# Converting float64 weights on chip in 512-column pieces, in place, with w_in's column groups as tiles of their own

## The chip, the cores and the metric

The kernel runs on one core of one Trainium2 chip. The metric is the device time of one execution in microseconds, as the median of several runs. A core has TensorE (PE in the profile), VectorE (DVE), ScalarE (ACT), GpSimd (POOL) and SyncE (SP), which here issues all transfers.

## The reference, cut to what matters

```python
def _attn_ref(q, k, v):                 # q, k, v: 8 batches, 8 heads, 576 positions, 64 columns, float32
    scores = scale * np.matmul(q, k.transpose(0, 1, 3, 2))
    mask = block_i >= block_j           # blocks of 64 positions
    scores = np.where(mask, scores, -1e9)
    ...                                 # softmax over the last axis
    return np.matmul(attn, v)

def _moe_ref(x, w_in, w_out):           # x: 4608 x 512, w_in: 512 x 2048, w_out: 2048 x 512
    h = x @ w_in
    g = np.where(h >= 1, h, np.where(h <= -1, 0.0, (h + 1) ** 2 / 4))
    return g @ w_out
```

x is the attention's result with the heads side by side. The two weight matrices come in as float64, 64 bits an element; q, k and v are float32.

## The kernel before

**Arithmetic.** TensorE multiplies operands of a rounded 32-bit type (`F32R`). To keep float32's precision the kernel splits each operand into a high part, the value rounded to `F32R`, and a low part, the rest, and adds up three products: high by high, high by low, low by high.

**Attention.** There are 32 pairs of heads (8 batches, 4 pairs each), and a pair is eight steps of `attention_steps`: scores and softmax of a group of positions, then, two steps after, the transposes of the probabilities (`turn`, `turn_last`), then the products with v. The steps of one pair run, in this order: scores (0, 0); scores (0, 1); scores (0, 2) and turn (0, 0); scores of the last block and turn (0, 1); scores (1, 0) and turn (0, 2); scores (1, 1) and the last block's turn; scores (1, 2), the product for head 0 and turn (1, 0); turn (1, 1) and the first product. The turn of (1, 2) and the second product come in the next pair's first two steps. From batch 3 on (`HOP = 3`) the probabilities (`pr`) hop: `as_float32r` copies them by DMA, SBUF to SBUF, into a tile `prr`, from which TensorE transposes them as `F32R`; the earlier batches transpose them as plain float32.

**Feed-forward.** The 4608 rows of x are 9 chunks of 512. For each chunk and each of 16 groups of 128 inner columns (`fc`) there is an `ffn_in` (12 matmuls at L626 into the one bank `ph`, then the activation at L635 to L641, which ends with GpSimd's subtraction for `gl`) and an `ffn_out` (12 matmuls at L650 and L655 into four banks `po`). At a chunk's end the four banks are copied to `ob` tiles, the even ones on VectorE (L665), the odd ones on ScalarE (L663), and stored (L667).

**The weights.** `convert` turns one piece of 128 rows by 256 columns from float64 to float32 and splits it. It is a generator in three parts, one part a call. The first loads the piece as pairs of 32-bit words into `bits`. ScalarE scales the high words, read as floats, into `top` (L164) and the low words in place (L165); VectorE clamps `top` (L166), shifts it into `mag` (L169) and adds the sign (L172). `top` and `mag` are the two halves of a tile `work`. In the second part GpSimd adds the low words to `mag` as integers (L178) and ScalarE copies it to the high part (L180). In the third GpSimd subtracts to get the low part (L182). w_in's parts stay in SBUF, in `wih` and `wil`; w_out's go through a tile `ws` to HBM (`wo_split`, L208), from where `ffn_in` loads them again (L643).

**Buffers.** `conv` has three tiles for `bits`, `conv2` three for `work`. The same six hold the hop's `prr` (columns up to 512 in `conv`, the last 64 of a row of 576 in `conv2`) and the `ob` tiles. Of the first 32 pieces, each second one borrows two tiles of the feed-forward (`t`, `gl`) in their place (`BORROW`).

**Order.** `weight_pieces` goes through w_in's columns 256 at a time: the four pieces of w_in, then the four of w_out's two row blocks that belong to these columns; 64 pieces in all. The loop at the kernel's end takes one attention step, then pieces, then one feed-forward step. Up to step `START` = 36 (batch 0 and four steps more) 24 pieces plus `LAG` = 2 are begun, then 5 for each 3 steps until all are; the feed-forward begins at START and takes one step (an `ffn_in` or an `ffn_out`) for each attention step. A scheduler then orders the instructions of each engine by priority, which follows this order. Counted so, the last `ffn_out` of chunk c falls on step 68 + 32c, and step number modulo 8 is the place in the pair.

## Time and profile before

| | us |
|---|---|
| runs | 1285.29, 1286.38, 1288.21; median 1286.38 |
| the profiled execution | 1285.23 |
| its span, first to last instruction | 1283.5 |
| TensorE busy | 1207.2 (94%) |
| VectorE busy | 888.4 (69%) |
| ScalarE busy | 766.3 (60%) |
| GpSimd busy | 472.2 (37%) |

A group's line in the profile gives the line of the kernel, the engine, the operation, output and inputs, the shapes, the count, then the busy time and the mean of one in ns, then the engine's idle time just before, with the releaser. The answer for one line of code gives the minimum, median and maximum of one in ns, and the starts of the first and the last. Rows of stretches give, for each engine in turn, busy time and count, then TensorE's granted clock, the share of the DMA engines and GB/s. A busy TensorE says little of how near it is to its peak, and an engine's busy time includes time in which a started instruction is held up.

### The profile page before, as it was taken

What the parts mean: (1) busy time and instruction counts of PE and PEld (TensorE: products, weight loads), DVE (VectorE), ACT (ScalarE), POOL (GpSimd) and SP (SyncE); (2) the same over time, 40 slices, a digit from 0 to 9 for tenths busy, and PEclk for the clock granted to TensorE, in tenths of its full rate; (3) what the DMA queues carried; (4) which work ended last, traced back from release to release, by engine and by line L of the source; (5) the groups of instructions that cost most, each with busy time, mean ns of one, the idle gap of its engine ahead of it and who ended that gap; (6) DMA issues with size and microseconds to landing.
All of it is one profiled execution on the core that took longest, in us unless ns stands there. A gap on an engine that the chain in (4) does not pass through costs nothing.

```text
span 1283.5 us, 20410 instructions
## 1 busy us (share of the span) xinstructions
PE 1207.2 (94%) x6496; PEld 1018.7 (79%) x6496; DVE 888.4 (69%) x2204; ACT 766.3 (60%) x1855; POOL 472.2 (37%) x466
## 2 busy tenths in 40 slices
PE   5877787899999999999999999999999999999998
PEld 4666665688888888888888888888888888888886
DVE  8998999877677777677777777777777767322222
ACT  6878676666666666666666666666666655322222
POOL 3545766633333333333333333333333332222222
PEclk9889999999999999999999999999999999999999
DMA  5656555434333545555444644464545443333432
GB/s 152 175 151 180 170 186 177 145 125 140 97 106 111 189 143 153 160 159 178 147 155 154 187 137 152 153 189 148 159 146 186 156 142 120 115 99 99 132 99 99
DMA packets 136812, 188.44 MB, mean 147 GB/s; under 512 B 61040, under 2 KB 87664, under 8 KB 136704
## 3 DMA queue, kind: packets, MB, share of 16 engines
q1 hardware_dynamic: 136704, 187.13, 47.2%
q8 instruction: 52, 0.85, 0.3%
q14 instruction: 56, 0.46, 0.1%
HBM read 120.59 MB, written 17.83 MB: 108 GB/s over the span
## 4 chain that ended last, share of the span: by engine, by line
PE 70%; DVE 13%; ACT 8%; issue 4%; DMA 2%; POOL 1%; SPq 1%; ACTq 0%; POOLq 0%; DVEq 0%
PE ph L626 26%; PE po L650 16%; PE po L655 8%; PE ps_av L480 7%; PE ps_s L371 3%; PE ps_s L374 3%; ACT pr L398 3%; PE ps_t L441 3%; PE ps_qk L327 2%; DVE pr L404 2%; ACT qb L331 2%; DVE nm L394 2%; DVE work L169 1%; PE ps_t L443 1%; DVE work L172 1%
## 5 line engine op out<-in xcount | busy, mean ns | idle before, releaser
L641 POOL TENSOR_TENSOR gl<-t,gh 128x512 fp32r<-128x512 f32 x144 | 187.2, 1300 | 577.5 <-ACT gh L640 310.8
L650 PE MATMUL po<-wo,gh 128*128 128x512 f32 x1152 | 299.7, 403 | 0.1
L650 PEld LDWEIGHTS po<-wo,gh 128*128 128x128 f32 x1152 | 210.6, 190 | 40.3 <-ACT gh L640 0.6
L626 PE MATMUL ph<-xh,wih 128*128 128x512 f32 x576 | 238.2, 414 | 1.7 <-DVE t L639 1.7
L636 DVE SCALAR_TENSOR_TENSOR t<-t 128x512 f32<-128x512 f32 x144 | 112.9, 784 | 183.1 <-ACT t L635 181.0
L626 PE MATMUL ph<-xl,wih 128*128 128x512 f32 x576 | 227.4, 395 | 1.1 <-DVE xl L516 1.1
L626 PE MATMUL ph<-xh,wil 128*128 128x512 f32 x576 | 227.9, 396 | 0.0
L635 ACT ACTIVATE t<-ph 128x512 f32<-128x512 f32 x144 | 86.0, 597 | 155.2 <-PE ph L626 155.2
L398 ACT ACTIVATE pr<-ps_s,nm 128x128 f32<-128x128 f32 (+3 forms) x256 | 134.2, 529 | 63.1 <-DVE nm L394 62.8
L655 PE MATMUL po<-wo,gl 128*128 128x512 f32 x576 | 155.4, 391 | 0.0
L394 DVE TENSOR_REDUCE nm<-ps_s 128x1 f32<-128x128 f32 (+3 forms) x256 | 123.6, 485 | 45.2 <-PE ps_s L374 43.6
L371 PE MATMUL ps_s<-ka,qa 68*128 68x288 f32 (+4 forms) x384 | 123.6, 336 | 20.5 <-ACT pr L398 12.8
L640 ACT CAST gh<-t 128x512 fp32r<-128x512 f32 x144 | 90.0, 625 | 84.6 <-DVE t L639 83.0
L626 PEld LDWEIGHTS ph<-xh,wil 128*128 128x128 f32 x576 | 109.4, 190 | 24.5
L434 ACT CAST pb<-ps_t 128x512 fp32r<-128x512 f32 (+1 forms) x140 | 77.5, 553 | 84.8 <-PE ps_t L441 65.5
L317 POOL TENSOR_TENSOR vsr<-vn,vsr 128x256 fp32r<-128x256 f32 (+1 forms) x112 | 82.9, 750 | 119.9 <-ACT vsr L316 119.9
L655 PEld LDWEIGHTS po<-wo,gl 128*128 128x128 f32 x576 | 108.4, 188 | 23.4
L626 PEld LDWEIGHTS ph<-xl,wih 128*128 128x128 f32 x576 | 109.9, 191 | 20.4 <-DVE xl L516 1.4
L626 PEld LDWEIGHTS ph<-xh,wih 128*128 128x128 f32 x576 | 109.4, 190 | 20.3 <-DVE t L639 2.0
L374 PE MATMUL ps_s<-kb,qb 128*128 128x288 f32 (+4 forms) x384 | 121.8, 323 | 0.0
L436 DVE TENSOR_TENSOR pb<-ps_t,pb 128x512 fp32r<-128x512 f32 (+1 forms) x140 | 88.1, 629 | 40.5 <-ACT pb L434 40.5
L404 DVE TENSOR_SCALAR pr<-pr,sm 128x128 f32<-128x128 f32 (+3 forms) x256 | 110.3, 451 | 3.6
(95 smaller groups left out, 2039.1 us busy)
## 6 DMA issues: line engine op xcount, KB each, us to landing
wo<-wo_split SPq DMA_DIRECT2D x144, 512.0 KB, 3.4
prr<-pr SPq DMA_DIRECT2D x80, 192.0 KB, 2.6
prr<-pr SPq DMA_DIRECT2D x60, 256.0 KB, 2.4
out_dram<-ob SPq DMA_DIRECT2D x36, 256.0 KB, 4.0
qn<-in_q_dram SPq DMA_DIRECT2D x32, 256.0 KB, 2.9
kn<-in_k_dram SPq DMA_DIRECT2D x32, 256.0 KB, 3.0
bits<-in_moe_w_in_dram SPq DMA_DIRECT2D x32, 256.0 KB, 3.1
bits<-in_moe_w_out_dram SPq DMA_DIRECT2D x32, 256.0 KB, 3.1
```

The lines of the kernel that those rows point to most:

```text
L371: nc.tensor.matmul(ps, qa[:KA, j, c0 : c0 + P], ka[:KA, j, k0 : k0 + n], start=first, stop=False)
L374: nc.tensor.matmul(ps, qb[:, j, c0 : c0 + P], kb[:, j, k0 : k0 + n], start=False, stop=last)
L394: nc.vector.tensor_reduce(out=nm[:, i : i + 1], in_=ps[:, cs], axis=AX.X, op=ALU.max, negate=True)
L398: nc.scalar.activation(pr[:, cs], ps[:, cs], AF.Exp, bias=nm[:, i : i + 1], scale=1.0, accum_out=sm[:, i : i + 1],)
L404: nc.vector.tensor_scalar_mul(pr[:, cs], pr[:, cs], sm[:, i : i + 1])
L480: nc.tensor.matmul(ps[:, lo_col:], vt, x, start=first and i == 0 and m == 0, stop=last and i == len(parts) - 1 and m == len(mov) - 1,)
L626: nc.tensor.matmul(ph, w[:, cc, fs], x[:, cc, xs], start=(cc == 0 and i == 0), stop=(cc == NCC - 1 and i == 2),)
L636: nc.vector.scalar_tensor_tensor(out=t_, in0=t_, scalar=1.0, in1=t_, op0=ALU.min, op1=ALU.mult)
L640: nc.scalar.copy(gh, t_)
L641: nc.gpsimd.tensor_tensor(out=gl, in0=t_, in1=gh.bitcast(F32), op=ALU.subtract)
L650: nc.tensor.matmul(po[tt], gh[:, ts_], wo[:, w, :], start=(fc == 0 and w == 0), stop=False)
L655: nc.tensor.matmul(po[tt], gl[:, ts_], wo[:, 0, :], start=False, stop=fc == NFC - 1)
```

## The change

A piece is now 512 columns wide (`CW`), so there are 32 pieces, eight for each of four groups (`NG`) of 512 columns of w_in: the four pieces of w_in, then the four of w_out that belong to them. `top` is no longer a tile of its own: ScalarE scales the high words where they are, so `top` is every second word of `bits` and is clamped there; only `mag` has another tile. w_in's parts are one pair of tiles for each column group. The last group's pair is allocated only when its first piece comes, in room that until then holds two more pairs of `bits` and `mag` (`early`), which each second piece uses; after that all pieces go through `conv`, which has two of each. The borrowed tiles and `conv2` are gone. The hop copies a row in one DMA, and its tiles, like the `ob` tiles, alternate between `conv`'s `bits` and `mag`, two of each; a row of 576 always takes a `bits`. Of the 32 pieces 12 plus `LAG` are begun by step START, then one a step.

```diff
@@ -52,9 +52,8 @@
     SCALE = 1.0 / float(D) ** 0.5
     MASKED = -1.0e9
     EPS = 1e-9
-    BORROW = 32
-
-    CW = 256
+    CW = 512
+    NG = DF // CW
     F32_TOP = float.fromhex("0x1.dffffcp-96")
     KA = D + NTL
     HOP = 3
@@ -65,8 +64,7 @@
     att3 = ctx.enter_context(tc.tile_pool(name="att3", bufs=3))
     small = ctx.enter_context(tc.tile_pool(name="small", bufs=6))
     ffn = ctx.enter_context(tc.tile_pool(name="ffn", bufs=2))
-    conv = ctx.enter_context(tc.tile_pool(name="conv", bufs=3))
-    conv2 = ctx.enter_context(tc.tile_pool(name="conv2", bufs=3))
+    conv = ctx.enter_context(tc.tile_pool(name="conv", bufs=2))
     dram = ctx.enter_context(tc.tile_pool(name="dram", bufs=1, space=bass.MemoryType.DRAM))
     ps_w = ctx.enter_context(tc.tile_pool(name="ps_w", bufs=3, space=bass.MemoryType.PSUM))
     ps_h = ctx.enter_context(tc.tile_pool(name="ps_h", bufs=1, space=bass.MemoryType.PSUM))
@@ -90,8 +88,22 @@
 
     xh = const.tile([P, NCC, RING], F32R, tag="xh", name="xh")
     xl = const.tile([P, NCC, RING], F32R, tag="xl", name="xl")
-    wih = const.tile([P, NCC, DF], F32R, tag="wih", name="wih")
-    wil = const.tile([P, NCC, DF], F32R, tag="wil", name="wil")
+
+
+    w_in_parts = [
+        [const.tile([P, NCC, CW], F32R, tag=f"wi{x}{g}", name=f"wi{x}{g}") for x in "hl"]
+        for g in range(NG - 1)
+    ]
+    late = {"pool": ctx.enter_context(ExitStack())}
+    late["early"] = late["pool"].enter_context(tc.tile_pool(name="early", bufs=2))
+
+    def open_last_group():
+        late["pool"].close()
+        late["early"] = None
+        last = ctx.enter_context(tc.tile_pool(name="last", bufs=1))
+        w_in_parts.append(
+            [last.tile([P, NCC, CW], F32R, tag=f"wi{x}", name=f"wi{x}") for x in "hl"]
+        )
     wo_split = dram.tile([NFC, P, 2, DM], F32, tag="wo_split", name="wo_split")
 
 
@@ -150,18 +162,14 @@
 
     def convert(n, source, hi, lo, done):
 
-        if n < BORROW and n % 2:
-            bits = ffn.tile([P, CW, 2], I32, tag="t", name="bits")
-            work = ffn.tile([P, 2, CW], F32, tag="gl", name="work")
-        else:
-            bits = conv.tile([P, CW, 2], I32, tag="bits", name="bits")
-            work = conv2.tile([P, 2, CW], F32, tag="work", name="work")
+        pool = late["early"] if n % 2 and late["early"] else conv
+        bits = pool.tile([P, CW, 2], I32, tag="bits", name="bits")
+        mag = pool.tile([P, CW], U32, tag="mag", name="mag")
         nc.sync.dma_start(bits, source.bitcast(I32).rearrange("p (n t) -> p n t", t=2))
-        top, mag = work[:, 0, :], work[:, 1, :].bitcast(U32)
-        low = bits[:, :, 0]
-
-
-        nc.scalar.mul(top, bits[:, :, 1].bitcast(F32), 2.0**-112)
+        top, low = bits[:, :, 1].bitcast(F32), bits[:, :, 0]
+
+
+        nc.scalar.mul(top, top, 2.0**-112)
         nc.scalar.mul(low, low.bitcast(U32), 2.0**-29)
         nc.vector.tensor_scalar(
             out=top, in0=top, scalar1=F32_TOP, scalar2=-F32_TOP, op0=ALU.min, op1=ALU.max
@@ -185,28 +193,27 @@
 
     def weight_pieces():
 
-        for f0 in range(0, DF, CW):
-            fs = slice(f0, f0 + CW)
+        for g in range(NG):
+            if g == NG - 1:
+                open_last_group()
             for cc in range(NCC):
                 yield (
-                    w_in[cc * P : (cc + 1) * P, fs],
-                    lambda cc=cc, fs=fs: wih[:, cc, fs], lambda cc=cc, fs=fs: wil[:, cc, fs], None,
-                )
-            for fc in range(f0 // P, (f0 + CW) // P):
+                    w_in[cc * P : (cc + 1) * P, g * CW : (g + 1) * CW],
+                    *(lambda cc=cc, part=part: part[:, cc, :] for part in w_in_parts[g]), None,
+                )
+            for fc in range(g * CW // P, (g + 1) * CW // P):
                 ws = {}
 
-                def part(w, d0, ws=ws):
+                def part(w, ws=ws):
                     if not ws:
                         ws[0] = ffn.tile([P, 2, DM], F32R, tag="wo", name="ws")
-                    return ws[0][:, w, d0 : d0 + CW]
-
-                for d0 in range(0, DM, CW):
-                    yield (
-                        w_out[fc * P : (fc + 1) * P, d0 : d0 + CW],
-                        lambda p_=part, d0=d0: p_(0, d0), lambda p_=part, d0=d0: p_(1, d0),
-                        None if d0 + CW < DM else
-                        lambda fc=fc, ws=ws: nc.sync.dma_start(wo_split[fc], ws[0].bitcast(F32)),
-                    )
+                    return ws[0][:, w, :]
+
+                yield (
+                    w_out[fc * P : (fc + 1) * P, :],
+                    lambda p_=part: p_(0), lambda p_=part: p_(1),
+                    lambda fc=fc, ws=ws: nc.sync.dma_start(wo_split[fc], ws[0].bitcast(F32)),
+                )
 
     def prepare_weights():
 
@@ -218,16 +225,18 @@
             live = [c for c in live if next(c, True) is None]
             yield
 
+    hops = {"n": 0}
+
     def as_float32r(src):
 
-        moved = []
-        for c0 in range(0, src.shape[1], TCH):
-            n = min(TCH, src.shape[1] - c0)
-            pool, tag = ((conv, "bits"), (conv2, "work"))[c0 > 0]
-            dst = pool.tile([P, TCH], F32R, tag=tag, name="prr")
-            nc.sync.dma_start(dst[:, :n].bitcast(F32), src[:, c0 : c0 + n])
-            moved.append(dst)
-        return moved
+        n = src.shape[1]
+        hops["n"] += 1
+        if n > TCH or hops["n"] % 2:
+            dst = conv.tile([P, 2 * TCH], F32R, tag="bits", name="prr")
+        else:
+            dst = conv.tile([P, TCH], F32R, tag="mag", name="prr")
+        nc.sync.dma_start(dst[:, :n].bitcast(F32), src)
+        return dst
 
 
     class Pair:
@@ -402,7 +411,7 @@
             self.inverse(sm[:, :m])
             for i, cs in enumerate(cols):
                 nc.vector.tensor_scalar_mul(pr[:, cs], pr[:, cs], sm[:, i : i + 1])
-            self.pr[j, g] = as_float32r(pr[:, : cols[-1].stop]) if self.hop else [pr]
+            self.pr[j, g] = as_float32r(pr[:, : cols[-1].stop]) if self.hop else pr
 
         def scores_last(self):
 
@@ -428,19 +437,18 @@
             nc.vector.tensor_tensor(out=sm[:, 2:3], in0=sm[:, 0:1], in1=sm[:, 1:2], op=ALU.add)
             self.inverse(sm[:, 2:3])
             nc.vector.tensor_scalar_mul(pr, pr, sm[:, 2:3])
-            self.pr["last"] = as_float32r(pr) if self.hop else [pr]
+            self.pr["last"] = as_float32r(pr) if self.hop else pr
 
         def split(self, ps, hi, lo=None):
             nc.scalar.copy(hi, ps)
             if lo is not None:
                 nc.vector.tensor_tensor(out=lo, in0=ps, in1=hi.bitcast(F32), op=ALU.subtract)
 
-        def transposed(self, out, parts, c0, n):
-            src = parts[c0 // TCH][:, c0 % TCH : c0 % TCH + n] if self.hop else parts[0][:, c0 : c0 + n]
+        def transposed(self, out, src, c0, n):
             if self.hop:
-                nc.tensor.transpose(out.bitcast(F32R), src, ident_r)
+                nc.tensor.transpose(out.bitcast(F32R), src[:, c0 : c0 + n], ident_r)
             else:
-                nc.tensor.transpose(out, src, ident)
+                nc.tensor.transpose(out, src[:, c0 : c0 + n], ident)
 
         def turn(self, j, g):
             tiles = self.GROUPS[g]
@@ -619,7 +627,9 @@
     def ffn_in(c, fc):
         at = (c * TCH) % RING
         ph = ps_h.tile([P, 512], F32, tag="ph", name="ph")
-        fs = slice(fc * P, (fc + 1) * P)
+        g, f0 = divmod(fc * P, CW)
+        fs = slice(f0, f0 + P)
+        wih, wil = w_in_parts[g]
         xs = slice(at, at + TCH)
         for cc in range(NCC):
             for i, (w, x) in enumerate(((wih, xh), (wih, xl), (wil, xh))):
@@ -656,9 +666,7 @@
         if fc < NFC - 1:
             return
         for tt in range(NTT):
-            ob = conv.tile([P, DM], F32, tag="bits", name="ob") if tt % 2 else conv2.tile(
-                [P, DM], F32, tag="work", name="ob"
-            )
+            ob = conv.tile([P, DM], F32, tag="bits" if tt % 2 else "mag", name="ob")
             if tt % 2:
                 nc.scalar.copy(ob, po[tt])
             else:
@@ -684,21 +692,13 @@
 
 
     START = 8 * NPAIR + 4
-    GROUP = CW // P
-    PART = NCC + GROUP * DM // CW
-    EARLY = 24
+    EARLY = 12
     LAG = 2
     weights = prepare_weights()
     ffn_steps = feed_forward()
     converted = 0
     for i, _ in enumerate(attention_steps()):
-        if i < START:
-            want = (i + 1) * EARLY // START
-        else:
-            want = max(
-                EARLY + (i - START + 1) * (NFC // GROUP * PART - EARLY) // (2 * NFC - 4 * GROUP),
-                ((i - START) // (2 * GROUP) + 1) * PART,
-            )
+        want = (i + 1) * EARLY // START if i < START else EARLY + i - START + 1
         want += LAG
         for _ in range(want - converted):
             next(weights, None)
```

## The prediction

> **What bounds the kernel now.** I read the page's 40 slices first, then the busy times by stage, then the chain of waits of the early stages, and last the groups by shape on VectorE, ScalarE and GpSimd.
>
> ```profile
> PE   5877787899999999999999999999999999999998
> DVE  8998999877677777677777777777777767322222
> ...
> 0.00:118.00 118.00, 84.99 (x446) 67.61 (x446) 103.25 (x309) 91.74 (x256) 55.52 (x76) 0.93 0.58 167
> 118.00:262.00 144.00, 112.61 (x545) 91.09 (x546) 132.15 (x296) 97.34 (x261) 94.00 (x106) 0.92 0.53 166
> 262.00:1100.00 838.00, 831.27 (x4725) 713.28 (x4725) 605.03 (x1531) 534.58 (x1270) 280.06 (x252) 1.00 0.48 149
> 1100.00:1283.50 183.50, 178.32 (x783) 146.74 (x781) 48.00 (x70) 42.67 (x71) 42.59 (x33) 0.99 0.34 109
> ...
> by line: issue 11.3%; DVE work L169 10.2%; DVE work L172 8.5%; POOL work L178 6.1%; DVE work L166 5.0%; DVE pr L404 4.9%; DVE t L636 3.9%; DVE nm L394 3.9%; PE ph L626 3.7%; ACT pr L398 3.1%; ACT work L164 3.0%; DVE t L639 3.0%; DVE pb L436
> ```
>
> The columns of the stage rows are TensorE, its weight loads, VectorE, ScalarE and GpSimd. There are two kernels in one. From 262 us on TensorE is busy 831 of 838 us: nothing that another engine saves there can show, and what is saved ahead of 262 us is kept to the end, since the same matmuls follow. Ahead of it VectorE is the full engine: 103.25 of 118 us up to the start of the feed-forward, 132.15 of the next 144. Of the chain in that second stretch the three conversion lines on VectorE (L166, L169, L172) are 24%, more than any engine's other work. These lines are what the change touches.
>
> ```profile
> L172 DVE SCALAR_TENSOR_TENSOR work<-work 128x256 uint32<-128x256 uint32 x64 | 37.0, 581 | 0.6
> L169 DVE TENSOR_SCALAR work<-work 128x256 uint32<-128x256 uint32 x64 | 32.2, 509 | 0.5
> L166 DVE TENSOR_SCALAR work<-work 128x256 f32<-128x256 f32 x64 | 27.8, 437 | 9.4 <-ACT work L164 9.3
> L404 DVE TENSOR_SCALAR pr<-pr,sm 128x512 f32<-128x512 f32 x15 | 13.0, 866 | 0.2
> ...
> L404 DVE TENSOR_SCALAR pr<-pr,sm 128x512 f32<-128x512 f32 x49 | 23.4, 478 | 0.8
> L291 DVE TENSOR_SCALAR qs<-qn 128x512 fp32r<-128x512 f32 x23 | 9.4, 409 | 0.0
> ...
> L166 DVE TENSOR_SCALAR work<-work x64: 264/286/1521, 10.3 to 250.5; 128x256 f32<-128x256 f32 x64
> L169 DVE TENSOR_SCALAR work<-work x64: 267/291/1534, 10.7 to 251.7; 128x256 uint32<-128x256 uint32 x64
> L172 DVE SCALAR_TENSOR_TENSOR work<-work x64: 397/416/1631, 13.3 to 253.5; 128x256 uint32<-128x256 uint32 x64
> L636 DVE SCALAR_TENSOR_TENSOR t<-t x144: 677/693/1390, 116.9 to 1273.3; 128x512 f32<-128x512 f32 x144
> ...
> 152.14 1.92 POOL L546 TENSOR_TENSOR xl<-x,xh 128x576 fp32r<-128x576 f32 x1
> 152.72 1.49 DVE L169 TENSOR_SCALAR work<-work 128x256 uint32<-128x256 uint32 x1
> ```
>
> The three lines cost 37.0 + 32.2 + 27.8 = 97.0 us, all ahead of 254 us. Their medians (286, 291, 416 ns) are far below their means. The last two rows say why: a 0.29 us L169 takes 1.49 us and ends when the GpSimd instruction beside it ends (152.14 + 1.92 = 154.06, 152.72 + 1.49 = 154.21). The same line L404 takes 866 ns (its first 15, ahead of 262 us) while GpSimd is full of conversions, and 478 ns (the 49 after that) once they are over. So a VectorE instruction here has a run, by its length, and a wait, by what GpSimd is doing. At the medians the runs are 64 x (0.286 + 0.291 + 0.416) = 63.6 us; the waits are the other 33.4 us, 0.174 us for each of 192.
>
> **VectorE, the term that pays.** 64 pieces of 256 columns become 32 of 512, so 192 instructions become 96. For a one-source run of 512 columns I take 0.41 us (L291, same kind, same width, 409 ns), for the two-source one 0.69 (L636, median). A piece costs 0.41 + 0.41 + 0.69 = 1.51 us, 32 cost 48.3 us: 15 us saved. GpSimd's own instructions get longer:
>
> ```profile
> L178 POOL TENSOR_TENSOR work<-work,bits 128x256 int32<-128x256 int32 x64 | 53.1, 833 | 65.6 <-ACT bits L165 12.4 <-DVE work L172 10.6 <-DVE sm L381 10.2
> L182 POOL TENSOR_TENSOR wil<-work,wih 128x256 fp32r<-128x256 f32 x32 | 27.0, 846 | 9.9 <-ACT wih L180 9.8
> L641 POOL TENSOR_TENSOR gl<-t,gh 128x512 fp32r<-128x512 f32 x12 | 16.6, 1386 | 15.4 <-ACT gh L640 15.2 <-DVE work L166 0.2
> ```
>
> At 1386 instead of 833 ns one wait may last up to 1.67 times as long, though GpSimd's other instructions do not change and its total falls (64 x 1.39 = 89 us for about 106). I take 1.4 times, 0.24 us, by 96: 23 us, 10 less than now. Together 71 us for 97: **26 us saved on VectorE**. If each wait stays at 0.174 us the saving is 32 us, and up to 37 with some of L404's waits gone as well. The lower end is for the new layout. "top" now stays in its tile, every second word (a step of 8 bytes), where it was packed in a tile of its own. No VectorE row shows that step. If it drops the one-source lines to the rate of the two-source one, 0.69 us, a piece runs 2.07 us, 32 run 66 us, and with waits of 1.67 x 0.174 = 0.29 us (28 us) the saving is only 3 us. I take the first price because of ScalarE, which works at that step already:
>
> ```profile
> L165 ACT ACTIVATE bits<-bits 128x256 int32<-128x256 uint32 x64 | 28.0, 442 | 2.0 <-DMA bits<-in_moe_w_in_dram 1.6 <-DMA bits<-in_moe_w_out_dram 0.3
> L164 ACT ACTIVATE work<-bits 128x256 f32<-128x256 f32 x64 | 28.0, 440 | 16.2 <-DMA bits<-in_moe_w_in_dram 9.6 <-POOL ws L182 5.6 <-DMA bits<-in_moe_w_out_dram 0.9
> L331 ACT CAST kb<-ps_qk 128x512 fp32r<-128x512 f32 x16 | 17.8, 1112 | 0.4 <-PE ps_qk L327 0.4
> L180 ACT CAST wih<-work 128x256 fp32r<-128x256 f32 x32 | 13.0, 409 | 15.6 <-POOL work L178 15.4
> L640 ACT CAST gh<-t 128x512 fp32r<-128x512 f32 x12 | 7.5, 628 | 0.9 <-DVE t L639 0.9
> ...
> L333 DVE CAST ka<-ps_qk x1: 1100/1100/1100, 12.4 to 12.4; 64x512 fp32r<-64x512 f32 x1
> ```
>
> L165 reads and writes every second word in place at 442 ns; packed L180 takes 409. A step of four words is another matter: L331 writes so and takes 1112 ns for 512 columns, and L333 does it on VectorE in 1100. So two words cost little, four cost a lot. [...]
>
> **What that is worth on the path.** VectorE is busy 235.4 of the first 262 us (90%), so I count 0.8 of a saved microsecond; the rest is lost where ScalarE's exponentials or TensorE end a chain. 26 x 0.8 = **21 us**.
>
> **ScalarE, GpSimd and the transfers, at nothing.** L164, L165 and L180's kind go from 64 x 1.29 us = 83 to 32 x about 1.94 = 62 us (L640's 628 ns for the copy, the other two taken as 0.03 more). ScalarE is at 189 of 262 us, so these 21 us are cover, not path. So are GpSimd's 17. SP issues 32 loads of weights for 64 and 140 hop copies for 160, and the bytes are the same; where the hop queue runs, TensorE is the bound.
>
> **The new waits.** The first 24 pieces go through four buffers, one piece a step once the feed-forward runs. The last 8 have two. There, the shift on VectorE into "mag" waits for GpSimd's subtraction of the piece two before; behind it queue that step's row maxima and L404, and TensorE's transposes wait for these. Six such waits of at most one GpSimd instruction are 8 us; with two steps between I take 0. The last group's tiles wait for the early buffers' readers: the last of these is piece 23's subtraction, which GpSimd's queue has ahead of piece 24 anyway: 0.
>
> In the hop part, "bits" has two buffers for three. A feed-forward chunk ends at step 68 + 32c, always the fifth step of a pair. In the five chunks that fall into the hop part both "bits" buffers then hold probabilities (the last block's and (1, 0)'s), so output tile 1 waits for the last block's transposes, as its ScalarE copy does now, and tile 3 for those of (1, 0):
>
> ```profile
> 709.83 1.06 ACT L663 COPY ob<-po 128x512 f32<-128x512 f32 x2
> ...
> 713.29 0.45 PE L441 MATMUL ps_t<-ident_r,prr 128*128 128x128 f32 x3
> 713.57 2.08 PE L650 MATMUL po<-wo,gh 128*128 128x512 f32 x8
> ```
>
> Those end at 713.74, the copy (1.06/2 us) could be done at 714.3, and the next chunk's seventh matmul, the first that needs tile 3's bank, comes at 713.57 + 6/8 x 2.08 = 715.1. I take 0; if ScalarE puts the copy behind other work, each burst costs up to the shift of 3.9 us (713.74 less 709.83), five cost 20 us.
>
> **The sum.** The profiled execution took 1285.23 us (span 1283.5 and 1.7 around it), 1.15 below the median of 1286.38. 1285.2 - 21 = 1264.2; on the median's scale 1265.4, so **1265 us**. What a measurement of this kernel can tell is about 0.2%, 2.6 us (the three runs spread over 2.9).
>
> **Rivals.**
> - The step of 8 bytes is dear on VectorE, and the kernel gets slower. Place: the successors of L166, L169 and L172. If each ran at L333's 1100 ns, 32 x 3 x 1.1 = 106 us and 23 of waits make 129 for 97: +32 x 0.8 = 25 us, **1311 us**. It decides from a mean, waits included, above 97.0/96 = 1.01 us an instruction. For: no row of VectorE excludes it. Against: ScalarE's two rows above. [...] Chance 0.09.
> - The saving doesn't reach the end of the stage. The two halves of a tile now interleave; if the first VectorE step has to wait for both ScalarE steps, it waits one 0.66 us instruction longer, and an in-order queue stands: 32 x 0.66 = 21 us, less 5 saved as L166's 9.4 us idle halves. Net gain (26 - 16) x 0.8 = 8 us, **1278 us**. For: L166 is the only conversion line that VectorE idles for now. Against: these ScalarE steps can be issued early. Chance 0.09.
> - The gain is made early and given back by the two-buffer hop queue: +20 us against -21, **1285 us**, no change; chance 0.06, and 0.06 more that it costs over that, some 1292 us. TensorE's 7 idle us in 838 speak against both: it is well ahead of its buffers now.
> - Main case: 0.70, own range 1249 to 1272 (a saving of 20 to 37 us counted at 0.7 to 1).
>
> **The numbers.** Faster: 0.70 + 0.09 = 0.79. Same: 0.06. Slower: 0.09 + 0.06 = 0.15. The range runs from 1247 (the main case's 37 us in full and 2 us of ScalarE's saving with it) to 1287 (the no-change case with its measurement); out of it are the slower cases and a few hundredths below.
>
> **What would show it.** Right: VectorE's three conversion groups at 128x512 x32 with medians near 410, 410 and 690 ns and a sum near 71 us; the last conversion ends near 235 us for 254; TensorE as full as now after that, and the later part as long. Wrong: medians near 1.1 us; idle time of VectorE on the second ScalarE step; TensorE gaps at the ends of chunks, released by an output copy. A shorter early part with a longer late part would be the third rival; an early part of the same length with a less busy VectorE would refute the reading that VectorE bounds it.

## The result and the profile after

The changed kernel takes 1294.35 us (median of 4 runs, 1292.26 to 1294.78), the kernel before 1285.84 beside it: ratio 1.0062, 95% interval 1.0042 to 1.0082. 1265 was predicted, with 1247 to 1287 as the range. The profiled execution after took 1292.26 us.

The page of the kernel after: span, busy times, and three of the rows in 40 slices.

```profile
span 1290.5 us, 20051 instructions
...
PE 1211.1 (94%) x6496; PEld 1023.0 (79%) x6496; DVE 882.0 (68%) x2108; ACT 760.1 (59%) x1759; POOL 459.8 (36%) x402
...
PE   4786777899999999999999999999999999999998
...
DVE  8888988777777777777777777777777777322222
...
PEclk9888888899999999999999999999999999999999
```

The busy times of the page before:

```profile
PE 1207.2 (94%) x6496; PEld 1018.7 (79%) x6496; DVE 888.4 (69%) x2204; ACT 766.3 (60%) x1855; POOL 472.2 (37%) x466
```

VectorE has 96 instructions fewer (2108 for 2204), yet its busy time falls only from 888.4 to 882.0 us. To see where the time went, both spans are cut at two marks: the first feed-forward activation (L635, now L645), and the first copy of an output tile on VectorE (L665, now L673). First the stretches before, then after (us, TensorE, its weight loads, VectorE, ScalarE, GpSimd, then TensorE's granted clock).

```profile
0.00:116.10 116.10, 84.00 (x440) 66.92 (x440) 101.58 (x304) 89.84 (x248) 55.52 (x76) 0.93 0.58 169
116.10:300.30 184.20, 151.53 (x767) 124.49 (x768) 161.54 (x373) 123.81 (x325) 106.09 (x117) 0.94 0.50 156
300.30:1283.50 983.20, 971.66 (x5291) 827.32 (x5289) 625.31 (x1530) 552.68 (x1284) 310.56 (x274) 1.00 0.46 143
```

```profile
0.00:126.80 126.80, 86.05 (x441) 69.14 (x442) 106.97 (x273) 91.51 (x216) 52.97 (x53) 0.89 0.55 164
126.80:307.90 181.10, 153.08 (x766) 126.54 (x767) 150.40 (x308) 114.74 (x262) 95.35 (x76) 0.91 0.48 152
307.90:1290.50 982.60, 971.99 (x5291) 827.34 (x5289) 624.59 (x1530) 553.82 (x1284) 311.45 (x274) 1.00 0.46 143
```

The late part is as long as before (982.6 for 983.2). All of the loss lies ahead of the first copy, which comes 7.6 us later (307.9 for 300.3). I call that part the early part, and split it in two: TensorE was busy for 239.1 us of it (86.05 + 153.08) where it was 235.5, for the same matmuls at a lower granted clock (0.89 and 0.91 for 0.93 and 0.94), and idle for 68.8 where it was 64.8. So 3.6 us are TensorE's own and 4.0 are waiting. The waiting changes in both directions: ahead of the first activation TensorE is idle 8.6 us longer (40.7 for 32.1), after it 4.7 us less (28.0 for 32.7). This is an accounting; which of these is a cause the experiments have to say.

The conversion lines did what was predicted of them. VectorE's groups of the kernel after, up to 262 us, then three of these lines by themselves (ns: minimum, median, maximum):

```profile
L180 DVE SCALAR_TENSOR_TENSOR mag<-bits,mag 128x512 uint32<-128x512 uint32 x32 | 27.3, 854 | 0.2
L177 DVE TENSOR_SCALAR mag<-bits 128x512 uint32<-128x512 uint32 x32 | 22.2, 695 | 0.9 <-POOL wil L190 0.5
L174 DVE TENSOR_SCALAR bits<-bits 128x512 f32<-128x512 f32 x32 | 21.2, 667 | 4.3 <-issue 3.0 <-ACT bits L172 1.2
L413 DVE TENSOR_SCALAR pr<-pr,sm 128x384 f32<-128x384 f32 x15 | 15.3, 1023 | 0.1
...
L413 DVE TENSOR_SCALAR pr<-pr,sm 128x512 f32<-128x512 f32 x14 | 9.9, 710 | 0.1
...
L174 DVE TENSOR_SCALAR bits<-bits x32: 402/419/1543, 12.2 to 236.4; 128x512 f32<-128x512 f32 x32
...
L177 DVE TENSOR_SCALAR mag<-bits x32: 407/419/1532, 12.6 to 240.1; 128x512 uint32<-128x512 uint32 x32
...
L180 DVE SCALAR_TENSOR_TENSOR mag<-bits,mag x32: 660/681/2193, 13.1 to 241.4; 128x512 uint32<-128x512 uint32 x32
```

The same stretch before had, for the softmax scaling of 384 columns:

```profile
L404 DVE TENSOR_SCALAR pr<-pr,sm 128x384 f32<-128x384 f32 x15 | 11.8, 784 | 0.0
```

The three lines sum to 27.3 + 22.2 + 21.2 = 70.7 us (97.0 before). But the softmax scaling, which the change doesn't touch, didn't get shorter with them. Its instructions of 384 columns now take 1023 ns for 784, those of 512 columns 710 for 866; that line's four widths together, ahead of 262 us, went from 40.3 to 42.4 us. Six rows of the timeline after, in three pairs, show what lengthens an instruction:

```profile
58.87 1.48 POOL L190 TENSOR_TENSOR ws<-mag,ws 128x512 fp32r<-128x512 f32 x1 [0.73 <-ACT ws L188]
59.14 1.43 DVE L413 TENSOR_SCALAR pr<-pr,sm 128x384 f32<-128x384 f32 x1
...
68.50 1.26 POOL L190 TENSOR_TENSOR ws<-mag,ws 128x512 fp32r<-128x512 f32 x1 [5.35 <-ACT ws L188]
...
68.81 1.00 DVE L310 CAST ks<-kn 128x64 fp32r<-128x64 f32 x1
...
73.26 1.30 POOL L186 TENSOR_TENSOR mag<-mag,bits 128x512 int32<-128x512 int32 x1 [1.22 <-DVE mag L180]
...
73.62 0.68 DVE L403 TENSOR_REDUCE nm<-ps_s 128x1 f32<-128x512 f32 x1
```

In the first two pairs VectorE's instruction started while GpSimd's ran and ended within 0.25 us of its end (60.57 against 60.35, 69.81 against 69.76); the cast of only 64 columns took 1.00 us. In the third it did not wait: the row maximum, which reads from one of the banks that TensorE writes (PSUM), took 0.68 us and was done before GpSimd (74.30 against 74.56). So a longer GpSimd instruction holds some of VectorE's instructions longer, those that work from SBUF to SBUF in these rows, and not others. The row maxima of 512 columns keep their mean of 688 ns from before to after.

### The profile page after: what moved, and what is told of

Same layout as the page of the kernel before. It is cut to its first block, busy times and chain, and to the rows that moved or that the text cites. A ratio compares the mean times of both kernels' runs of the same rounds, so it can differ in the third digit from the quotient of the medians.

```text
span 1290.5 us, 20051 instructions
## 1 busy us (share of the span) xinstructions
PE 1211.1 (94%) x6496; PEld 1023.0 (79%) x6496; DVE 882.0 (68%) x2108; ACT 760.1 (59%) x1759; POOL 459.8 (36%) x402
## 4 chain that ended last, share of the span: by engine, by line
PE 73%; DVE 12%; ACT 6%; issue 4%; DMA 2%; POOL 2%; SPq 1%; ACTq 0%; DVEq 0%; POOLq 0%
PE ph L636 27%; PE po L660 17%; PE po L665 8%; PE ps_av L488 7%; PE ps_s L380 3%; PE ps_s L383 3%; DVE pr L413 3%; PE ps_t L449 3%; ACT pr L407 3%; PE ps_qk L336 2%; DVE nm L403 2%; PE ps_t L451 2%; ACT qb L340 2%; DVE sm L389 1%; DVE mag L180 1%
## 5 line engine op out<-in xcount | busy, mean ns | idle before, releaser
L646 DVE SCALAR_TENSOR_TENSOR t<-t 128x512 f32<-128x512 f32 x144 | 115.7, 804 | 186.8 <-ACT t L645 184.8
L645 ACT ACTIVATE t<-ph 128x512 f32<-128x512 f32 x144 | 86.0, 597 | 160.8 <-PE ph L636 160.8
L407 ACT ACTIVATE pr<-ps_s,nm 128x128 f32<-128x128 f32 (+3 forms) x256 | 134.2, 528 | 61.9 <-DVE nm L403 61.5
L665 PE MATMUL po<-wo,gl 128*128 128x512 f32 x576 | 155.3, 391 | 0.0
L326 POOL TENSOR_TENSOR vsr<-vn,vsr 128x256 fp32r<-128x256 f32 (+1 forms) x112 | 87.0, 787 | 126.5 <-ACT vsr L325 126.5
L636 PEld LDWEIGHTS ph<-xh,wil 128*128 128x128 f32 x576 | 109.8, 191 | 24.7
L636 PEld LDWEIGHTS ph<-xh,wih 128*128 128x128 f32 x576 | 109.9, 191 | 21.6 <-DVE sm L389 2.9
L665 PEld LDWEIGHTS po<-wo,gl 128*128 128x128 f32 x576 | 108.4, 188 | 23.3
L413 DVE TENSOR_SCALAR pr<-pr,sm 128x128 f32<-128x128 f32 (+3 forms) x256 | 112.9, 462 | 3.7
```

The costliest lines, as they stand in the source:

```text
L407: nc.scalar.activation(pr[:, cs], ps[:, cs], AF.Exp, bias=nm[:, i : i + 1], scale=1.0, accum_out=sm[:, i : i + 1],)
L413: nc.vector.tensor_scalar_mul(pr[:, cs], pr[:, cs], sm[:, i : i + 1])
L636: nc.tensor.matmul(ph, w[:, cc, fs], x[:, cc, xs], start=(cc == 0 and i == 0), stop=(cc == NCC - 1 and i == 2),)
L646: nc.vector.scalar_tensor_tensor(out=t_, in0=t_, scalar=1.0, in1=t_, op0=ALU.min, op1=ALU.mult)
L665: nc.tensor.matmul(po[tt], gl[:, ts_], wo[:, 0, :], start=False, stop=fc == NFC - 1)
```

## The experiments

Each kernel is told by where its early part ends, and by TensorE's busy and idle time in it. "256" and "512" are the kernels before and after. Times are medians; the ratio is to the kernel before, run beside it. The three columns ahead of the median are of one profiled execution, which lies within 2.2 us of the median but for two: that of "512, pace of 256" took 1293.02 us, 4.5 below its median, and that of "the same, more buffers" 1298.28, 5.1 above. "Other parity" is explained under "The order alone".

| kernel | first copy | TensorE busy | idle | median | ratio (95%) |
|---|---|---|---|---|---|
| 256 | 300.3 | 235.5 | 64.8 | 1285.84 | |
| 256, other parity | 308.9 | 242.8 | 66.1 | 1293.31 | 1.0065 (1.0050 to 1.0080) |
| 256, `top` in place | 300.8 | 235.1 | 65.7 | 1287.63 | 1.0017 (1.0005 to 1.0028) |
| 256, pace of 512 | 307.6 | 240.3 | 67.3 | 1291.69 | 1.0046 (1.0033 to 1.0060) |
| 256, no shift | 295.6 | 237.9 | 57.8 | 1282.63 | 0.9985 (0.9971 to 0.9998) |
| 256, no addition | 287.8 | 233.8 | 54.0 | 1272.38 | 0.9897 (0.9882 to 0.9912) |
| 256, no addition, no low scaling | 282.2 | 231.0 | 51.2 | 1265.74 | 0.9851 (0.9827 to 0.9875) |
| 512 | 307.9 | 239.1 | 68.8 | 1294.35 | 1.0062 (1.0042 to 1.0082) |
| 512, other parity | 303.6 | 238.7 | 64.9 | 1289.91 | 1.0031 (1.0018 to 1.0044) |
| 512, pace of 256 | 308.7 | 243.9 | 64.8 | 1297.51 | 1.0088 (1.0066 to 1.0110) |
| new layout, 256 wide | 309.5 | 243.2 | 66.3 | 1297.02 | 1.0088 (1.0072 to 1.0103) |
| the same, more buffers | 308.5 | 244.5 | 64.0 | 1293.15 | 1.0058 (1.0041 to 1.0075) |
| 512, GpSimd in halves | 297.9 | 236.0 | 61.9 | 1285.94 | 1.0006 (0.9996 to 1.0017) |
| the same, other parity | 299.4 | 238.8 | 60.6 | 1287.13 | 1.0013 (1.0002 to 1.0024) |
| halves, fewer early pieces | 304.1 | 238.0 | 66.2 | 1293.07 | 1.0057 (1.0039 to 1.0075) |
| 256, subtraction on VectorE | 294.5 | 235.7 | 58.8 | 1279.67 | 0.9964 (0.9950 to 0.9977) |
| the same, other parity | 298.3 | 240.0 | 58.3 | 1283.76 | 0.9983 (0.9972 to 0.9994) |
| 512, subtraction on VectorE | 283.6 | 232.2 | 51.4 | 1270.30 | 0.9891 (0.9876 to 0.9906) |
| the same, other parity | 289.2 | 235.4 | 53.8 | 1275.80 | 0.9925 (0.9897 to 0.9952) |
| the same as two rows up, addition in halves | 286.2 | 235.4 | 50.8 | 1273.96 | 0.9914 (0.9899 to 0.9928) |

In all of them the rest, from the first copy to the end, is 982 to 988 us long.

### Long GpSimd instructions, or the pace, or the layout

The first theory was that GpSimd's longer instructions hold VectorE. The edit on the kernel after:

```
-        nc.gpsimd.tensor_tensor(out=w32, in0=w32, in1=low, op=ALU.add)
+        for h in (slice(0, CW // 2), slice(CW // 2, CW)):
+            nc.gpsimd.tensor_tensor(out=w32[:, h], in0=w32[:, h], in1=low[:, h], op=ALU.add)
...
+        for h in (slice(0, CW // 2), slice(CW // 2, CW)):
+            nc.gpsimd.tensor_tensor(
+                out=lo()[:, h], in0=w32[:, h], in1=hi()[:, h].bitcast(F32), op=ALU.subtract
+            )
```

> The changed kernel with its two GpSimd instructions of each piece (the integer addition and the subtraction) issued as two of 256 columns each; all else as changed. Theory A (the longer GpSimd instructions hold up VectorE's attention instructions): the softmax scaling of 128x384 in the first 129 us falls from 1314 ns to about 920, the feed-forward starts near 120 us for 129, and the time comes back to 1286 us or below. Theory B (pace: 28 of 64 units of 256 columns are begun by the start of the feed-forward for 26, and two units a step after it for 1.67): no change, 1294 us. Theory C (pieces twice as long stand in the in-order queues of ScalarE and VectorE ahead of the attention's instructions): no change or a little slower by the 64 extra GpSimd instructions, 1294 to 1297 us. Theory D (the new layout: in place, four buffers, group tiles): 1294 us.

The page, the early part and the 384-column scaling (up to 262 us) of this kernel:

```profile
PE 1208.2 (94%) x6496; PEld 1019.6 (80%) x6496; DVE 863.7 (67%) x2108; ACT 758.5 (59%) x1759; POOL 476.2 (37%) x466
...
0.00:297.90 297.90, 235.97 (x1206) 192.36 (x1207) 239.26 (x578) 204.77 (x476) 164.82 (x193) 0.91 0.53 162
...
L417 DVE TENSOR_SCALAR pr<-pr,sm 128x384 f32<-128x384 f32 x15 | 8.6, 572 | 0.2
```

The hold is as the theory has it: the scaling is down from 1023 to 572 ns, and VectorE is busy 24.7 us less than before the change (863.7 for 888.4), nearly the 26 us that I had forecast. Yet the time is that of the kernel before, 1.0006: the saving was delivered, and against the kernel before it bought nothing. Two things limit what this says. The comparison has the rest of the change in it, layout and pace, whose cost may hide a gain. Against the kernel after, 18.1 us off VectorE's early part (257.4 to 239.3, the sum of its two stretches above) brought 8.4 us, the time that theory A forecast, but less than half of what was saved. And the order of VectorE's instructions changed too; the same halves in another order, below, brought 2.8 us.

Two kernels tried the other suspects. The first has the layout of the kernel after with pieces of 256 columns, in the order and pace of the kernel before. The second is the kernel before with 28 of its pieces begun by START and then two a step:

```
+    PW = CW // 2
...
+        bits = pool.tile([P, PW, 2], I32, tag="bits", name="bits")
+        mag = pool.tile([P, PW], U32, tag="mag", name="mag")
```

```
-    EARLY = 24
+    EARLY = 26
...
+        want = (i + 1) * EARLY // START if i < START else EARLY + 2 * (i - START + 1)
```

> The changed kernel's layout (top in place, the early buffers in the last group's room, group tiles, one-copy hop) with pieces of 256 columns, in the order and at the pace of the kernel before. Theory A and theory C: 1286 us or up to 10 below, the feed-forward starts near 118 us. Theory B: 1286 us as well, since the pace is the old one. Theory D: stays at 1294 us.

> The kernel before with the changed kernel's pace alone: 28 units of 256 columns begun by the start of the feed-forward for 26, then two a step. Theory B: most of the loss is here, 1290 to 1294 us, with the feed-forward starting near 125 us. Theories A, C, D: 1284 to 1288 us.

Both are slower than before, by 0.88% (1297.02, above what any theory gave) and 0.46%, though neither converts in long GpSimd instructions. If the pace were the cause, the kernel after at the pace of before should have gained, and the halved one with a smaller start too (`EARLY = 9` for 12):

```
-    EARLY = 12
+    EARLY = 11
...
-        want = (i + 1) * EARLY // START if i < START else EARLY + i - START + 1
+        want = (i + 1) * EARLY // START if i < START else EARLY + (i - START + 1) * 20 // 24
```

> The changed kernel at the pace of the kernel before (26 units of 256 columns begun by the start of the feed-forward, then 1.67 a step). Theory B: back to 1286 us, start of the feed-forward near 119 us. Theories A, C, D: 1292 to 1295 us; the start a microsecond or two earlier than 129 us, given back after it.

> The changed kernel with GpSimd's two instructions in halves, and 11 pieces instead of 14 begun by the start of the feed-forward (the number EARLY 9 for 12), one a step after it. If each unit of 256 columns ahead of that start costs 2.7 us, as the run with the new pace suggests (5.4 us for two), the start comes 10 to 16 us earlier than 121 us, and the time is 1278 to 1284 us if the later stretch does not take it all back. If the place of the conversions does not matter, 1286 us.

Neither did (1297.51 and 1293.07, the latter outside both forecasts). So theory B's range held for the run that added the pace (1291.69) and failed for the one that took it out. By idle time alone the kernel after at the old pace is at 64.8 us for 68.8, but so is it with nothing but the buffers exchanged (64.9). Whether the pace costs some microseconds stays open. More buffers for the new layout with narrow pieces, and the in-place `top` alone, put into the kernel before, were the next two:

```
+    late["early"] = late["pool"].enter_context(tc.tile_pool(name="early", bufs=5))
...
+        pool = late["early"] if n % 7 > 1 and late["early"] else conv
```

```
-        top, mag = work[:, 0, :], work[:, 1, :].bitcast(U32)
+        top, mag = bits[:, :, 1].bitcast(F32), work[:, 1, :].bitcast(U32)
...
+        nc.scalar.mul(top, top, 2.0**-112)
```

> The run with the new layout and pieces of 256 columns, which took 1297 us, with seven pairs of buffers instead of four until the last group opens (five in the last group's room, two in the pool of the hop). If the number of buffers is what made the new layout slow there (four of 256 columns hold half of what four of 512 hold, and the old kernel had five), 1284 to 1290 us; if not, 1293 to 1298 us.

> The kernel before with one part of the change: top stays in place, every second word of the loaded tile; pieces of 256 columns, buffers and pace as before (391 of VectorE's instructions stand elsewhere, 4 of TensorE's). If working in place is what makes the new layout slow (the run with the new layout and 256 columns took 1297 us): 1290 to 1297 us. If it is the buffers or nothing of the layout: 1283 to 1288 us. Theory O: in between is possible.

With more buffers 4 of 12 us came back, which is the upper of the two forecasts, "if not"; in place cost 0.17%. The new layout with narrow pieces costs more than the whole change, and the parts tried don't add up to it, which suggests that something else varies between these kernels.

### What a saved microsecond is worth

Three kernels take work out of the kernel before, one step each: VectorE's shift (L169), GpSimd's addition (L178), and with it ScalarE's scaling of the low words (L165).

```
-        nc.vector.tensor_scalar(
-            out=mag, in0=top.bitcast(U32), scalar1=3, scalar2=None, op0=ALU.logical_shift_left
-        )
...
-            out=mag, in0=top.bitcast(U32), scalar=0x80000000, in1=mag,
+            out=mag, in0=top.bitcast(U32), scalar=0x80000000, in1=top.bitcast(U32),
```

```
-        nc.gpsimd.tensor_tensor(out=w32, in0=w32, in1=low, op=ALU.add)
```

```
-        nc.scalar.mul(low, low.bitcast(U32), 2.0**-29)
```

> The kernel before without VectorE's shift (L169) of each piece: 32.2 us of VectorE's time in 64 instructions are left out, and the converted weights are not the right ones. Theory P (VectorE is the bound of the first 262 us, as the prediction read it, 0.8 of each microsecond): 1286 - 26 = 1260 us. Theory Q (the early part is a chain through several engines, in which VectorE's time counts for little by itself): 1276 to 1284 us.

> The kernel before without GpSimd's integer addition (L178): 53.1 us of GpSimd's time are left out, and with them part of VectorE's waits on it. Theory R (GpSimd's instructions, by holding up VectorE and by their place in the conversion's chain, set the early part): 1260 us or below, with a saving larger than that of the shift. Theory P: VectorE's waits fall by about half of 33 us for the conversion and of 17 us for the softmax scaling, 25 us by 0.8: 1266 us. Theory Q: 1275 to 1283 us.

> As the run without the addition, and also without ScalarE's scaling of the low words (L165), 28.0 us of ScalarE's time, which only the addition reads. Read against that run. Theories P and R: within 3 us of it. Theory Q: 5 to 15 us below it.

The page and the early part without the shift, then without the addition, then the early part without the low scaling too:

```profile
PE 1209.5 (95%) x6496; PEld 1022.6 (80%) x6496; DVE 863.7 (68%) x2140; ACT 767.2 (60%) x1855; POOL 469.1 (37%) x466
...
0.00:295.60 295.60, 237.85 (x1206) 195.44 (x1207) 240.59 (x611) 214.59 (x572) 158.27 (x193) 0.90 0.54 163
```

```profile
PE 1205.0 (95%) x6496; PEld 1019.4 (80%) x6496; DVE 871.2 (69%) x2204; ACT 766.7 (60%) x1855; POOL 421.2 (33%) x402
...
0.00:287.80 287.80, 233.80 (x1206) 191.90 (x1207) 246.36 (x674) 213.99 (x572) 110.30 (x129) 0.93 0.55 168
```

```profile
0.00:282.20 282.20, 231.00 (x1206) 191.22 (x1207) 236.59 (x674) 193.50 (x508) 111.60 (x129) 0.93 0.56 171
```

Without the shift VectorE is again 24.7 us less busy, and the kernel 2 us faster (0.9985). TensorE's idle time falls by 7.0 us; 2.3 of these come back as a longer busy time. So a microsecond of VectorE's is worth 0.1 in time and 0.28 in idle, not 0.8. The time of this kernel lies where theory Q put it. The addition, 51 us of GpSimd's (472.2 less 421.2 by the pages), brings 12.4 us, with 16.8 us off VectorE's busy time in the early part beside it. The low scaling, 20.5 us of ScalarE's early part (213.99 to 193.50), brings 6.6 more; the early part of the profiled execution is 5.6 us shorter, half of it idle time (54.0 to 51.2) and half TensorE's busy time. No engine's work is the path by itself in these runs. GpSimd's and ScalarE's, which I had set at nothing, pay a quarter to a third of what is taken out, and VectorE's shorter waits are in the quarter. Each of the three was run in one order alone, and the next section shows that an order can move some 8 us: the addition's 12.4 us is more than that, the other two gains are not. But for the shift to have been worth 0.8, some 20 us, the order would have had to hide 18.

### The order alone

Exchanging which pieces take which of two sets of buffers, the odd ones or the even ones ("other parity" in the table), leaves the instructions and the buffers the same. What changes is the order that the scheduler finds, and which piece waits for which buffer:

```
-        pool = late["early"] if n % 2 and late["early"] else conv
+        pool = late["early"] if n % 2 == 0 and late["early"] else conv
```

It was done in the kernel after, in the halved one, and (with `BORROW`) in the one before.

> The changed kernel with the two kinds of buffers exchanged (even pieces take the early buffers, odd ones the pool of the hop): the same work, the same buffers, but 168 of VectorE's 2110 instructions stand elsewhere in its queue and 4 of TensorE's 6442. This is about as far from the changed kernel's order as the run with GpSimd's instructions in halves (191 and 6). Theory A (the long GpSimd instructions cost the 8 us): 1292 to 1296 us, as the changed kernel. Theory O (the early part depends on the order that the scheduler happens to choose, and the halves only brought a better order): anywhere from 1283 to 1300 us, away from 1294.

> The run with GpSimd's instructions in halves, with the same exchange of buffers (22 of VectorE's instructions stand elsewhere). Theory A: 1284 to 1288 us. Theory O: may lie anywhere from 1283 to 1297 us.

> The kernel before with its borrowed buffers given to the even pieces instead of the odd ones: the same work, 139 of VectorE's instructions elsewhere and 23 of TensorE's. It says how much an order alone moves the kernel before. Theory A: 1283 to 1288 us. Theory O: 1280 to 1297 us, most likely slower than 1287.

The early parts of before and after with the exchange:

```profile
0.00:308.90 308.90, 242.77 (x1206) 197.91 (x1207) 263.62 (x675) 213.69 (x572) 159.34 (x193) 0.90 0.51 156
```

```profile
0.00:303.60 303.60, 238.70 (x1206) 197.15 (x1207) 255.06 (x578) 205.92 (x476) 149.58 (x129) 0.90 0.52 159
```

And the halved one with the exchange:

```profile
0.00:299.40 299.40, 238.80 (x1207) 196.46 (x1207) 239.61 (x579) 205.01 (x476) 166.02 (x193) 0.89 0.53 161
```

The kernel before became 7.7 us slower and the one after 4.4 faster; exchanged, before and after have changed places. So the order is worth as much as the whole result. What it moves is in the rows: in the kernel before, TensorE's idle time stays (66.1 for 64.8), and its busy time for the same matmuls rises by 7.2 us, as its granted clock falls from 0.93 to 0.90. In the kernel after it is the idle time that moves, by 3.9 us. The clock also varies between executions of one kernel: of the 23 of the kernel before that ran beside this one, four were granted 0.974 or 0.975 over the whole span and took 1287.43 to 1289.95 us, the others 0.978 to 0.984 and 1282.21 to 1286.83; the exchanged kernel was granted 0.971 to 0.974 in all four of its own. The idle time is the steadier measure: in the four kernels of 256 columns that leave nothing out and have the subtraction on GpSimd, in the old layout, it is 64.8 to 67.3, in the three of 512, 64.8 to 68.8.

The kernel after and the halved one, both with the exchange, are also the cleanest pair for the price of VectorE's time. They have the same layout and pace and run in nearly the same order (in their traces 2093 of VectorE's 2108 instructions and 6495 of TensorE's 6496 stand in the same sequence). The halves take 15.5 us off VectorE's early part (255.06 to 239.61) and bring 2.8 us (1289.91 to 1287.13), 0.2 of each microsecond. GpSimd is busy 16.4 us longer for it; if these cost the quarter found above, VectorE's price would be 0.4. So the 8.4 us that the halves brought in the first order were in part the order.

### The subtraction off GpSimd

If GpSimd's instructions both hold VectorE and delay what is queued behind them, then one of them moved to VectorE should pay, and more at 512 columns. The edit, in the kernel before and in the one after, and then with the addition in halves besides:

```
-        nc.gpsimd.tensor_tensor(out=lo(), in0=w32, in1=hi().bitcast(F32), op=ALU.subtract)
+        nc.vector.tensor_tensor(out=lo(), in0=w32, in1=hi().bitcast(F32), op=ALU.subtract)
```

> The kernel before with the last subtraction of each piece (L182) on VectorE instead of GpSimd: about 64 x 0.42 = 27 us more of VectorE's own work, 53 us less on GpSimd. Theory S (in the early part GpSimd's instructions cost, by holding up VectorE and as a link of the conversion, 0.23 us a microsecond as the run without the addition showed; VectorE's cost 0.07 as the run without the shift showed): -12 + 2 = -10, 1275 us, up to 1282. Theory P (VectorE's time is the bound): +27 less some 25 of waits, by 0.8: 1285 to 1290 us.

> The changed kernel with the last subtraction of each piece (L190) on VectorE; the addition stays on GpSimd in one instruction of 512 columns. Theory S: half of the long GpSimd instructions are gone; half of the 8 us that halving them gave, and 0.23 x 42 us of GpSimd's time: 1280 to 1288 us. Theory P: 32 x 0.69 = 22 us more on VectorE, 1294 us or above.

> As the run before this one, and the addition on GpSimd in two halves of 256 columns. Theory S: another 3 to 5 us, 1275 to 1284 us, the fastest of the changed kernel's variants. Theory P: 1290 us or above.

Then the exchange of buffers in the first two, to see whether the order had made their gains:

> The 256-column kernel with the low part's subtraction on VectorE, its borrowed buffers going to the even pieces in place of the odd ones: the same work in another order. Theory W (the subtraction on VectorE is itself worth some microseconds, and 512 columns are worth some more once GpSimd is relieved of it): below the kernel before, 1276 to 1284 us, first output copy at 290 to 297 us. Theory O (the gains of both kernels with the subtraction on VectorE lie in the order that the scheduler happened to find): anywhere within 8 us of 1279.7, so above 1284 as easily as not.

> The 512-column kernel with the subtraction on VectorE, the early buffers going to the even pieces: the same work in another order. Theory W: 1268 to 1276 us, at least 4 us below the 256-column kernel beside it, first output copy at 281 to 288 us. Theory O: 1275 to 1282 us, and the distance to the 256-column kernel gone or turned round.

The kernel after with the subtraction on VectorE: page, early part, and VectorE's groups up to 262 us.

```profile
PE 1204.4 (95%) x6496; PEld 1018.1 (80%) x6496; DVE 873.0 (69%) x2140; ACT 759.4 (60%) x1759; POOL 421.9 (33%) x370
...
0.00:283.60 283.60, 232.16 (x1206) 190.55 (x1207) 248.46 (x611) 205.04 (x476) 110.30 (x97) 0.93 0.56 170
...
L180 DVE SCALAR_TENSOR_TENSOR mag<-bits,mag 128x512 uint32<-128x512 uint32 x32 | 21.8, 682 | 0.1
L174 DVE TENSOR_SCALAR bits<-bits 128x512 f32<-128x512 f32 x32 | 18.5, 581 | 2.9 <-ACT bits L172 2.9
L177 DVE TENSOR_SCALAR mag<-bits 128x512 uint32<-128x512 uint32 x32 | 17.0, 533 | 0.2
...
L190 DVE TENSOR_TENSOR ws<-mag,ws 128x512 fp32r<-128x512 f32 x16 | 12.9, 808 | 2.0 <-ACT ws L188 2.0
...
L190 DVE TENSOR_TENSOR wil<-mag,wih 128x512 fp32r<-128x512 f32 x16 | 12.0, 747 | 1.4 <-ACT wih L188 1.4
```

VectorE has 32 instructions more, 24.9 us of them, and is busy for less than without them (873.0 for 882.0): the three conversion lines alone fall from 70.7 to 57.3 us, with GpSimd's long subtractions gone. Now the change pays. At 256 columns the idle time is 58.8 and 58.3 us in the two orders, at 512 it is 51.4 and 53.8, and the medians are 1279.67 and 1283.76 against 1270.30 and 1275.80: 8 to 9 us between the two kernels in either order, more than the 4 to 6 us that the exchange moves. These two differ by the whole change, width, layout and pace; which part pays was not tried. Theory W's times held in both orders (its first copies came 1.2 to 1.3 us later than forecast); theory S's range held at 256 columns (1279.67) and missed at 512 (1280 to 1288 for 1270.30). That one is the fastest of those that leave nothing out, 1.1% faster than before the change (0.9891).

Halving the addition on top of it gains nothing: 1273.96, where theory S had the fastest of all. The order of the other engines' instructions is the same there, VectorE's early part is 6.6 us less busy (248.46 to 241.90), idle time is 50.8 for 51.4, and TensorE is busy 3.3 us longer at a clock of 0.91 for 0.93. So a less busy VectorE bought nothing here either.

## Why the prediction was wrong, step by step

- **What is saved early is kept; the late part stays.** Held: 983.2 and 982.6 us. The hop with two buffers and the output copies cost nothing, so that rival falls.
- **VectorE's conversion lines, 97 to 71 us.** Held: 70.7, with medians of 419, 419 and 681 ns for the 410, 410 and 690 forecast. The step of 8 bytes costs nothing that these medians show, and the first rival falls. The last of these instructions starts at 241.4 us (253.5 before), where 235 was forecast for the end of the conversions.
- **26 us off VectorE.** Only 6.4 came (888.4 to 882.0). This step failed. I had let the conversion lines wait longer for GpSimd, but not the other instructions of the early part; I had even put a possible gain there. Added up from the trace, the durations of VectorE's other instructions ahead of the first copy grew by some 13 us (206 to 220). And a sum of durations, which the 26 us were, is not busy time, since VectorE's instructions overlap in the records: all durations together fell by some 13 us (304 to 291), the busy time of that part by only 5.7 (263.1 to 257.4).
- **0.8 of a saved microsecond reaches the path.** This step failed too, and would have failed with the 26 us in hand: the kernel without the shift, with 24.7 us less on VectorE, took 2 us less (0.9985), and in the exchanged order 15.5 us less on VectorE brought 2.8. The halves in the first order brought the most, 8.4 us for 18.1. So these three show 0.1 to 0.5 of each microsecond, not 0.8. "Busy 90%" was partly the hold by GpSimd. My reading of the rest, argued and not shown, is that the early part is a set of chains that run through ScalarE, GpSimd and TensorE in turn, where a shorter link leaves another one last.
- **ScalarE's and GpSimd's savings at nothing.** Wrong in the other direction: taken out one after the other, such savings paid a quarter to a third, in one order.
- **VectorE waits for the second ScalarE step** (the second rival): L174 idled 4.3 us, 1.2 of them for ScalarE. It falls.
- **New waits from fewer buffers.** L177's wait for GpSimd's subtraction is 0.5 us: nothing, as forecast.

I had written that an early part of the same length with a less busy VectorE would refute the bound; the halved kernel is just that (297.9 us with 239.3 of VectorE, for 300.3 with 263.1), with the rest of the change in it.

What stays open: the sign. The forecast gain of 21 us is shown not to exist. But at 0.8 even the 6.4 us that came would have made the kernel 5 us faster, and it is 8.5 us slower; no run shows what makes up that difference. An exchange of buffers moved 4 to 8 us in four kernels of five (1.2 in the halved one), so the order can be a good part of it. Nor is it settled why TensorE is granted a lower clock in one order than in another (its early busy time ranges from 231.0 to 244.5 us in the table), nor why the new layout with narrow pieces has among the longest of these.

## What to carry to other kernels

An engine that is 90% busy is the bound only if taking work off it moves the time: try that with one step left out before pricing a saving (here 24.7 us off VectorE brought 2). Where GpSimd and VectorE share a stage, look at the median against the mean of VectorE's instructions, and count a GpSimd instruction's length on every VectorE line that such instructions are seen to hold, not only on the lines being changed. Add up busy time by windows rather than by groups, since a group's durations can overlap with another's (here VectorE's add up to 304 us in 263.1 us of busy time ahead of the first copy). And before believing a gain or a loss below 1% in a scheduled kernel, exchange two buffers of one kind and see how far the order alone moves it (here by 1.2 to 7.7 us, up to 0.6%).

## What the runs showed of the hardware

- Some VectorE instructions that begin beside one of GpSimd's end with it: 1.00 us for a cast of 64 columns, 0.05 us past GpSimd's end, where the shortest of that line took 0.17. Others are not held: a row maximum read from PSUM took 0.68 us beside one of GpSimd's of 1.30. In these pairs the held ones work from SBUF to SBUF, and the row maximum has a single input, in PSUM; no run shows what decides it. Of the size of the hold one pair of kernels says something: moving 43.5 us of subtractions (21.9 + 21.6 in the rows below) to VectorE made VectorE 9 us less busy (873.0 for 882.0), its order changing as well.

GpSimd's groups of the kernel after, up to 307.9 us:

```profile
L190 POOL TENSOR_TENSOR ws<-mag,ws 128x512 fp32r<-128x512 f32 x16 | 21.9, 1371 | 24.9 <-ACT ws L188 21.2 <-DMA bits<-in_moe_w_out_dram 2.3 <-DVE sm L390 1.4
L190 POOL TENSOR_TENSOR wil<-mag,wih 128x512 fp32r<-128x512 f32 x16 | 21.6, 1357 | 8.8 <-ACT wih L188 7.6 <-DMA qn<-in_q_dram 1.2
```

- The same subtraction is 1371 and 1357 ns on GpSimd, and 808 and 747 on VectorE with its holds.
- TensorE's granted clock is 1.00 where it is 99% busy (971.99 of 982.6 us) and 0.89 to 0.94 in the early stretches of the kernels before and after, where it is 68 to 85% busy. The early stretches don't rank by that share (0.93 at 72%, 0.91 at 85%), and two kernels with about the same idle time in the early part (58.8 and 58.3 us), the kernel before with the subtraction on VectorE in its two orders, were granted 0.93 and 0.90 there:

```profile
0.00:294.50 294.50, 235.73 (x1206) 191.47 (x1207) 262.15 (x739) 214.83 (x572) 112.55 (x129) 0.93 0.54 164
...
0.00:298.30 298.30, 240.04 (x1206) 196.64 (x1207) 263.39 (x738) 215.29 (x572) 111.03 (x129) 0.90 0.53 162
```
